# Building the decay mask of a retention kernel with two stacked float32r products instead of eight float32 ones

## The chip, the core and the metric

The kernel runs on one core of a Trainium2 chip. The core has a matrix engine (PE, with its weight loads shown apart as PEld), a vector engine (DVE), an activation engine (ACT), a general engine (POOL) and a sync engine (SP) that mostly issues DMAs; ACT issues some DMAs too. Each engine takes its instructions in program order. The metric is device time in microseconds (us) of one launch; lower is better. Chunks are counted from 0 below.

## The reference

The computation is a chain: retention (a linear attention with a decay per head), a gated feed-forward block, and four experts.

```python
# retention: B=2, H=8, S=768, D=64
gamma = 1.0 - 2.0 ** (-5.0 - np.arange(H))
for t in range(S):
    state = gamma * state + outer(k[:, :, t], v[:, :, t])
    y[:, :, t] = (1 / sqrt(D)) * q[:, :, t] @ state
# tokens: 1536, d_model 512
xn = x / rms(x) * rms_g
x = (silu(xn @ w_gate) * (xn @ w_val)) @ w_out                  # d_ff 1536, weights in float64
out = sum_e p[:, e] * (relu(x @ w1[e]) @ w2[e])                 # 4 experts, 1024 wide
```

## The kernel before

Retention runs over 12 chunks of 128 tokens (two batches of six). For a chunk the kernel computes the scores k·q of all eight heads (`scores`, L645: eight float32 matmuls, pairs of heads on the two halves of the rows), multiplies them on DVE by a decay mask (`masked`, L652), and multiplies the result with v (`mix`, L673); from chunk 1 of a batch on, `mix` also adds q times the running state (L665). At the end of `mix` the state gains k times v (L701), and ACT copies it to SBUF (L709). A chunk's q has to be multiplied by a table of decays before L665 (`prep_q`, L634, on POOL or DVE); that table, `gq`, is the product of `picks` and `q_rows` (L868), which ACT casts from constants (L859, L860), and ACT copies the product from PSUM (L870).

The mask is made once, before chunk 0. Mask[j, i] for a head is gamma^-j times gamma^i / sqrt(D) where i ≥ j. `rows` holds the two factors on a single partition; eight float32 matmuls with one row each (L832) form the outer products, and DVE multiplies them by the triangle `causal`, half of the constant `square` (L834). Around this PE also multiplies a tile of zeros by itself: eight times at the very start (L826), and eight times between the scores of chunk 0 and those of chunk 1 (L862).

The weights arrive as float64 and are turned into float32 pieces on ACT, DVE and POOL (L312 to L382) in the gaps of the retention stage. What runs when on ACT, DVE, POOL and SP there is set by a planner in Python (`Pace`): it keeps a model time `pace.now`, a clock for each engine and a cost for each operation, and at each `fill` issues the waiting tasks that fit. Whatever changes its model time or the place of a call changes which task goes to which engine, and in which order. DMAs are issued from SP in program order, and a few at the start from ACT. A DMA takes one of eight completion semaphores in turn (`DMAHW0` to `DMAHW7`), and its issue waits until the DMA before it on the same semaphore has landed.

## Time and profile before

| | |
|---|---|
| runs | 865.54, 866.02, 867.91 us; median 866.02 |
| profiled execution | span 865.7 us |
| PE busy | 853.1 us, 99% of the span |
| DVE busy | 574.6 us, 66% |
| ACT busy | 378.3 us, 44% |
| POOL busy | 280.8 us, 32% |
| mean DMA rate | 61 GB/s |

The profile is one execution. Its page gives the busy time of each engine, the span in slices, the chain of work that ended last, and groups of instructions; the timeline lists the instructions with start and duration. A float32 matmul appears as two records, so eight matmuls are "x16", and the end of a matmul in these records lies some tenths of a microsecond behind the start of the next. The column PEclk gives the granted share of PE's clock; it reads 1.00 in every stretch of this execution, but equal matmuls last twice as long in the first 14 us as after them, so which level the engine ran at is read from durations.

### The profile page before, as it was taken

Reading aid. Unit: us, or ns where it says so; the run is one execution under the profiler, and the core shown is the slowest. Engines: PE = TensorE matmul, PEld = TensorE weight load, DVE = VectorE, ACT = ScalarE, POOL = GpSimd, SP = SyncE. Lnnn points to the kernel's source line nnn. Section 1 sums busy time; section 2 is a strip of 40 time slices with the busy share of each in tenths; the row PEclk is TensorE's granted clock in tenths of the full one; section 3 lists DMA queues with packets and bytes.
Section 4 is the critical chain, followed back from the end, with each engine's and each line's share of the span. In section 5 each row is a group of like instructions: output and inputs, shape, how many; then the busy total and the mean of one; then the engine's idle time right before and its main releaser. Section 6 shows DMA issues by size and latency. Waiting matters only on the chain.

```text
span 865.7 us, 12619 instructions
## 1 busy us (share of the span) xinstructions
PE 853.1 (99%) x4731; PEld 793.1 (92%) x4731; DVE 574.6 (66%) x1054; ACT 378.3 (44%) x845; POOL 280.8 (32%) x354
## 2 busy tenths in 40 slices
PE   9999999999999999999999999999999999999998
PEld 8889999999999999889889998999889988999887
DVE  3987878979977876943565556556656566555554
ACT  3877766444354456655333233333233333333221
POOL 1366666525244458551122012012012112201000
PEclk9999999999999999999999999999999999999999
DMA  7763133211213111101011011001001101101003
GB/s 228 252 196 106 50 98 95 69 57 49 74 50 93 54 56 30 37 25 37 13 49 37 15 48 48 26 25 50 25 25 49 37 12 49 37 17 46 25 10 137
DMA packets 32749, 52.74 MB, mean 61 GB/s; under 512 B 4358, under 2 KB 13446, under 8 KB 32688
## 3 DMA queue, kind: packets, MB, share of 16 engines
q1 hardware_dynamic: 32480, 51.70, 19.1%
q8 instruction: 37, 0.61, 0.3%
q10 hardware_dynamic: 208, 0.23, 0.1%
q14 instruction: 24, 0.20, 0.1%
HBM read 48.78 MB, written 3.15 MB: 60 GB/s over the span
## 4 chain that ended last, share of the span: by engine, by line
PE 88%; DVE 5%; ACT 3%; POOL 2%; issue 1%; DMA 0%; DVEq 0%; ACTq 0%; SPq 0%; POOLq 0%
PE bank L460 41%; PE bank L1069 10%; PE bank L1070 10%; PE bank L1068 10%; PE bank L1001 3%; PE bank L1002 3%; PE bank L1000 3%; PE bank L673 1%; DVE s L553 1%; PE bank L665 1%; POOL x2Tlo L953 1%; PE bank L645 1%; DVE kept L550 1%; PE state L701 1%; DMA kn<-in_kn_dram 0%
## 5 line engine op out<-in xcount | busy, mean ns | idle before, releaser
L1076 DVE SCALAR_TENSOR_TENSOR oacc<-bank,p_sb,oacc 128x512 f32<-128x512 f32 (+1 forms) x181 | 134.8, 745 | 67.7 <-PE bank L1070 67.7
L1069 PE MATMUL bank<-plainlo,hs 128*128 128x512 f32 (+1 forms) x386 | 151.5, 392 | 0.0
L1070 PE MATMUL bank<-plainhi,hs 128*128 128x512 f32 (+1 forms) x386 | 151.5, 392 | 0.0
L1068 PE MATMUL bank<-plainhi,hs 128*128 128x512 f32 (+1 forms) x386 | 150.7, 391 | 0.0
L469 ACT COPY kept<-bank 128x384 f32<-128x384 f32 x168 | 80.5, 479 | 153.6 <-PE bank L460 151.4
L1033 DVE TENSOR_TENSOR kept<-bank,kept 128x384 f32<-128x384 f32 x96 | 53.5, 557 | 119.4 <-PE bank L460 88.2
L382 POOL TENSOR_TENSOR plainlo<-wst,plainhi 128x512 fp32r<-128x512 f32 x16 | 27.8, 1737 | 284.8 <-ACT plainhi L377 284.8
L1070 PEld LDWEIGHTS bank<-plainhi,hs 128*128 128x128 f32 x386 | 72.5, 188 | 16.1
L460 PE MATMUL bank<-x2Thi,widehi 128*128 128x384 f32 x256 | 86.2, 337 | 0.7 <-DVE kept L1033 0.7
L460 PE MATMUL bank<-x2Thi,widelo 128*128 128x384 f32 x256 | 85.7, 335 | 0.0
L460 PE MATMUL bank<-x2Tlo,widehi 128*128 128x384 f32 x256 | 85.7, 335 | 0.0
L1069 PEld LDWEIGHTS bank<-plainlo,hs 128*128 128x128 f32 x386 | 72.4, 188 | 14.3 <-POOL plainlo L382 0.3
L1068 PEld LDWEIGHTS bank<-plainhi,hs 128*128 128x128 f32 x386 | 72.4, 188 | 14.0
L382 POOL TENSOR_TENSOR widelo<-sums,widehi 128x512 fp32r<-128x512 f32 x37 | 48.4, 1308 | 112.7 <-ACT widehi L377 112.3
L1036 ACT ACTIVATE hs<-kept 128x384 fp32r<-128x384 f32 x96 | 50.4, 525 | 76.8 <-DVE kept L1033 76.8
L1001 PE MATMUL bank<-hlo,plainhi 128*128 128x384 f32 x192 | 64.3, 335 | 1.1 <-POOL hlo L558 1.0
L460 PE MATMUL bank<-xThi,widehi 128*128 128x384 f32 x192 | 64.6, 337 | 0.0
L460 PE MATMUL bank<-xThi,widelo 128*128 128x384 f32 x192 | 64.3, 335 | 0.0
L1002 PE MATMUL bank<-hhi,plainlo 128*128 128x384 f32 x192 | 64.2, 335 | 0.0
L1000 PE MATMUL bank<-hhi,plainhi 128*128 128x384 f32 x192 | 64.2, 334 | 0.0
L460 PE MATMUL bank<-xTlo,widehi 128*128 128x384 f32 x192 | 64.2, 334 | 0.0
L558 POOL TENSOR_TENSOR hlo<-s,hhi 128x384 fp32r<-128x384 f32 x44 | 47.0, 1071 | 33.5 <-ACT hhi L555 26.8
(155 smaller groups left out, 1924.2 us busy)
## 6 DMA issues: line engine op xcount, KB each, us to landing
wst<-in_moe_w_dram SPq DMA_DIRECT2D x64, 256.0 KB, 2.8
wst<-in_moe_w_gate_dram SPq DMA_DIRECT2D x12, 512.0 KB, 3.8
wst<-in_moe_w_val_dram SPq DMA_DIRECT2D x12, 512.0 KB, 3.7
wst<-in_moe_w_out_dram SPq DMA_DIRECT2D x12, 512.0 KB, 3.2
v<-in_vn_dram SPq DMA_DIRECT2D x12, 256.0 KB, 3.7
kn<-in_kn_dram SPq DMA_DIRECT2D x12, 256.0 KB, 4.1
q<-in_qt_dram SPq DMA_DIRECT2D x11, 256.0 KB, 4.3
k<-in_kt_dram SPq DMA_DIRECT2D x11, 256.0 KB, 3.0
```

The lines of the kernel that those rows point to most:

```text
L382: eng.tensor_tensor(out=at(lo), in0=t, in1=at(hi).bitcast(F32), op=ALU.subtract)
L460: nc.tensor.matmul(out=ps, lhsT=lhs, rhs=rhs, start=(first and j == i == 0), stop=(j == KH - 1 and i == 2), skip_group_check=not first,)
L469: nc.scalar.copy(out=t, in_=ps)
L1000: nc.tensor.matmul(out=ps, lhsT=whi[:, c], rhs=hi, start=(f == 0), stop=False)
L1001: nc.tensor.matmul(out=ps, lhsT=whi[:, c], rhs=lo, start=False, stop=False)
L1002: nc.tensor.matmul(out=ps, lhsT=wlo[:, c], rhs=hi, start=False, stop=(f == NF - 1))
L1033: nc.vector.tensor_tensor(out=t, in0=a, in1=t, op=ALU.add)
L1036: 0, "A", TB, lambda eng: eng.activation(out=hi, in_=t, func=AF.Relu), [pace.done(end)]
L1068: nc.tensor.matmul(out=ps, lhsT=hi[:, c], rhs=whi[:, cols], start=(f == 0), stop=False)
L1069: nc.tensor.matmul(out=ps, lhsT=hi[:, c], rhs=wlo[:, cols], start=False, stop=False)
L1070: nc.tensor.matmul(out=ps, lhsT=lo[:, c], rhs=whi[:, cols], start=False, stop=(f == NF - 1))
L1076: nc.vector.scalar_tensor_tensor(out=acc, in0=ps, scalar=pe, in1=acc, op0=ALU.mult, op1=ALU.add)
```

## The change

The two factor rows of the eight heads are split into a high and a low part and laid out on 16 rows (four pairs of heads, four products of parts); `right` holds zeros outside the pair's own columns, so one matmul over 16 rows with 512 columns gives four heads' tables at once, in float32r. DVE casts the right side in two instructions and ACT the left side in one. Only the triangle is sent early; the identity, the other half of `square`, is sent after the constants of the q table. The zero matmuls become ten before the table and three behind it; the eight between the first two chunks' scores go. The casts of `q_rows` and `picks`, and the q table of chunk 1 with `prep_q(1)`, move behind `mix(0)`. The planner's start time goes from 6.0 to 5.0.

```diff
-    WARM = 8
+    WARM = 10
+    MORE = 3
...
-        rows = [wstage.tile([P, H, CHUNK], F32, tag="wst", name=f"rows{x}")[0:1] for x in range(2)]
+        right, left = (wstage.tile([P, 2, NP, CHUNK], F32, tag="wst", name=nm)[0:NL] for nm in ("right", "left"))
+        left = left[:, :, 0]
+        rights = ap2.tile([P, 2, NP, CHUNK], F32R, tag="am", name="rights")[0:NL]
+        lefts = ap2.tile([P, NP, CHUNK], F32R, tag="xn", name="lefts")[0:NL, 0:2]
...
+        def tables(i):
+            if i < NCH - 1:
+                ps = pairs(bank())
+                nc.tensor.matmul(out=ps, lhsT=picks[:, i], rhs=q_rows, start=True, stop=True)
+                pace.matmuls(0.23)
+                nc.scalar.copy(out=gq[:, i], in_=ps)
+                gq_end[i] = pace.did("A", DM)
+            prep_q(i + 1)
...
-        for x in range(2):
-            nc.scalar.dma_start(out=rows[x], in_=c_rows[:, x])
+        nc.scalar.dma_start(out=right, in_=c_right)
+        nc.scalar.dma_start(out=left, in_=c_left)
+        nc.scalar.dma_start(out=causal, in_=c_square[:, 1])
         load(0, "q")
         load(0, "k")
-        nc.scalar.dma_start(out=square, in_=c_square)
...
         nc.scalar.dma_start(out=flat[:, NP:NP + NCH - 1], in_=c_pick)
+        nc.scalar.dma_start(out=ident, in_=c_square[:, 0])
...
+        nc.scalar.copy(out=lefts, in_=left)
+        nc.vector.tensor_copy(out=rights[:, 0], in_=right[:, 0])
+        nc.vector.tensor_copy(out=rights[:, 1], in_=right[:, 1])
         decays = [pairs(bank()) for j in range(2)]
-        for n in range(NP):
-            for j in range(2):
-                h = 2 * n + j
-                nc.tensor.matmul(out=decays[j][:, n, :], lhsT=rows[0][:, h], rhs=rows[1][:, h], start=True, stop=True)
+        for j in range(2):
+            nc.tensor.matmul(out=decays[j], lhsT=lefts[:, j], rhs=rights[:, j], start=True, stop=True)
+        for n in range(MORE):
+            nc.tensor.matmul(out=idle[:, 0, :], lhsT=S_sb[0][:, 0, :], rhs=S_sb[0][:, 0, :], start=True, stop=True)
...
-        pace.now = 6.0
+        pace.now = 5.0
...
-            if i == 0:
-
-                nc.scalar.copy(out=q_rows, in_=flat[:, 0:NP])
-                nc.scalar.copy(out=picks, in_=flat[:, NP:NP + NCH - 1])
-                for n in range(8):
-                    nc.tensor.matmul(out=idle[:, 0, :], lhsT=S_sb[0][:, 0, :], rhs=S_sb[0][:, 0, :], start=True, stop=True)
...
             mix(i)
+            if i == 0:
+                nc.scalar.copy(out=q_rows, in_=flat[:, 0:NP])
+                nc.scalar.copy(out=picks, in_=flat[:, NP:NP + NCH - 1])
+                tables(i)
```

How instructions stand before, on ACT from its first DMA to the first state copies of chunk 0 (`rows_q` is the tile that the q table's two constants are loaded to, `xn,ss` the square sum of chunk 0):

```order
L803 DMA rows_112<-in_c_rows_dram 1x1024
L803 DMA rows_113<-in_c_rows_dram 1x1024
L806 DMA square<-in_c_square_dram 128x256 [waits DMAHW2_49]
L809 DMA rows_q<-in_c_q_dram 20x512 [waits DMAHW4_49]
L810 DMA rows_q<-in_c_pick_dram 20x640 [waits DMAHW6_49]
L859 CAST q_rows<-rows_q 20x512 [waits DMAHW4_49]
L860 CAST picks<-rows_q 20x640 [waits DMAHW6_49]
L870 COPY gq<-bank 128x512 [waits PE_49]
L687 ACTIVATE xn,ss<-bank 128x512 [waits PE_49]
L689 ACTIVATE r_239<-ss,eps 128x1 [waits Activation_49]
L691 ACTIVATE vv<-ss,less 128x1 [waits Pool_49]
L709 COPY S_121<-state 64x4x64 [waits DVE_49,PE_49]
```

The same stretch of ACT in the changed kernel, up to the copy of the first q table:

```order
L817 DMA right<-in_c_right_dram 16x1024
L818 DMA left<-in_c_left_dram 16x2x128
L819 DMA square<-in_c_square_dram 128x128 [waits DMAHW1_49]
L824 DMA rows_q<-in_c_q_dram 20x512 [waits DMAHW3_49]
L825 DMA rows_q<-in_c_pick_dram 20x640 [waits DMAHW5_49]
L826 DMA square<-in_c_square_dram 128x128 [waits DMAHW7_49]
L844 CAST lefts<-left 16x256
...
L724 COPY S_123<-state 64x4x64 [waits DVE_49,PE_49]
L724 COPY S_123<-state 64x4x64
L887 CAST q_rows<-rows_q 20x512 [waits DMAHW3_49]
L888 CAST picks<-rows_q 20x640 [waits DMAHW5_49]
L660 COPY gq<-bank 128x512 [waits PE_49]
```

The cast of the left side stands behind four DMA issues, each of which waits for an earlier DMA, and the casts for the q table have moved from ahead of chunk 0's square sum to behind its state copies.

PE before, from the start to the product of the state of chunk 0:

```order
L826 MATMUL bank<-S_121 128x128 [waits DVE_49]
L826 MATMUL bank<-S_121 128x128 x7
L832 MATMUL bank<-rows_113,rows_112 128x128 [waits DMAHW7_49,DMAHW4_49]
L832 MATMUL bank<-rows_113,rows_112 128x128 x7
...
L862 MATMUL bank<-S_121 128x128 x8
L645 MATMUL bank<-q,k 128x128 [waits DMAHW1_49,DMAHW0_49]
L645 MATMUL bank<-q,k 128x128 [waits DVE_49]
L645 MATMUL bank<-q,k 128x128 x6
L868 MATMUL bank<-q_rows,picks 128x512 [waits DVE_49,Activation_49]
L673 MATMUL bank<-v,am 128x64 [waits DMAHW5_49,DVE_49]
```

PE in the changed kernel, the start and then from the product with v of chunk 0 to the scores of chunk 2:

```order
L842 MATMUL bank<-S_123 128x128 [waits DVE_49]
L842 MATMUL bank<-S_123 128x128 x9
L849 MATMUL bank<-rights,lefts 128x512 [waits DVE_49,Activation_49]
L849 MATMUL bank<-rights,lefts 128x512 [waits DVE_49]
L851 MATMUL bank<-S_123 128x128 x3
...
L688 MATMUL bank<-v,am 128x64 x6
L716 MATMUL state<-v,kn 128x128 [waits DMAHW4_49,Pool_49]
L716 MATMUL state<-v,kn 128x128 x3
L658 MATMUL bank<-q_rows,picks 128x512 [waits Activation_49]
L651 MATMUL bank<-q,k 128x128 [waits DMAHW3_49,DMAHW2_49,PE_49]
```

The first q-table product now stands between the state product of chunk 0 and the scores of chunk 2, and waits for ACT there. Elsewhere PE's rows keep their order; on DVE, ACT, POOL and SP the tasks of the planner change places through the retention stage.

## Rows read from the trace of the kernel before

**Rows 1.** The page: the span, and busy us, share and instructions of each engine.
```profile
span 865.7 us, 12619 instructions
PE 853.1 (99%) x4731; PEld 793.1 (92%) x4731; DVE 574.6 (66%) x1054; ACT 378.3 (44%) x845; POOL 280.8 (32%) x354
```
**Rows 2.** Timeline, PE: start us, us, engine, line, output and inputs, records.
```profile
1.45 3.78 PE L826 MATMUL bank<-S 128*128 128x128 f32 x16 [1.45 <-DVE S L811]
5.16 3.78 PE L832 MATMUL bank<-rows,rows 1*128 1x128 f32 x16
8.87 2.08 PE L645 MATMUL bank<-q,k 64*128 64x128 f32 x16
10.88 3.66 PE L862 MATMUL bank<-S 128*128 128x128 f32 x16
14.46 1.16 PE L645 MATMUL bank<-q,k 64*128 64x128 f32 x16
15.56 0.49 PE L868 MATMUL bank<-q_rows,picks 20*128 20x512 f32 x1
15.97 2.00 PE L673 MATMUL bank<-v,am 128*128 128x64 f32 x16
17.81 1.11 PE L701 MATMUL state<-v,kn 128*128 128x128 f32 x8
18.85 1.16 PE L645 MATMUL bank<-q,k 64*128 64x128 f32 x16
20.36 0.49 PE L665 MATMUL bank<-S,q 128*128 128x128 f32 x2
```
**Rows 3.** Timeline, the queues of ACT and SP: start and length of DMA issues.
```profile
3.98 0.38 ACTq L806 DMA_DIRECT2D square<-in_c_square_dram  x1
5.72 0.33 SPq L818 DMA_DIRECT2D g_sb<-in_moe_rms_g_dram  x1
5.95 0.29 ACTq L810 DMA_DIRECT2D rows_q<-in_c_pick_dram  x1
```
**Rows 4.** Timeline, ACT, DVE and POOL around the first two chunks.
```profile
8.65 0.62 ACT L859 CAST q_rows<-rows_q 20x512 fp32r<-20x512 f32 x1 [6.42 <-DMA rows_q<-in_c_q_dram]
10.59 0.73 ACT L860 CAST picks<-rows_q 20x640 fp32r<-20x640 f32 x1 [1.32 <-DMA rows_q<-in_c_pick_dram]
10.98 1.29 DVE L652 TENSOR_TENSOR am<-bank,mask 128x512 f32<-128x512 f32 x2 [1.14 <-PE bank L645]
16.08 0.58 ACT L870 COPY gq<-bank 128x512 f32<-128x512 f32 x1 [4.76 <-PE bank L868]
16.74 1.27 POOL L634 TENSOR_TENSOR q<-q,gq 128x512 f32<-128x512 f32 x1 [6.17 <-ACT gq L870]
19.12 0.73 ACT L709 COPY S<-state 64x256 f32<-64x256 f32 x2
```
**Rows 5.** Busy us by stretch: PE, PEld, DVE, ACT, POOL; then PEclk, DMA share, GB/s.
```profile
2.00:4.00 2.00, 2.00 (x12) 2.00 (x11) 0.00 (x0) 0.21 (x2) 0.00 (x0) 1.00 0.96 262
20.00:30.00 10.00, 10.00 (x91) 9.23 (x90) 9.32 (x17) 8.43 (x25) 4.60 (x6) 1.00 0.78 225
30.00:40.00 10.00, 9.58 (x92) 8.43 (x90) 9.09 (x19) 8.13 (x25) 2.41 (x2) 1.00 0.75 241
40.00:60.00 20.00, 18.22 (x182) 16.87 (x182) 17.09 (x37) 15.15 (x46) 11.41 (x16) 1.00 0.69 232
80.00:100.00 20.00, 19.22 (x110) 17.89 (x109) 14.52 (x25) 14.91 (x34) 15.13 (x14) 1.00 0.09 27
```
**Rows 6.** The chain that ended last, in order of time: start, us, what.
```profile
29.99 4.17 DMA kn<-in_kn_dram
34.18 0.69 DVE kn L623
38.06 0.46 PE bank L665 x2
```

## The prediction

> **What bounds the kernel now.** I read the engine totals first, then the timeline of the first 22 us, then the stretches of the retention stage, then the chain. PE is busy for 853.1 of 865.7 us [rows 1]; the reader should see there that only two things can move the time: work that leaves PE, and holes between PE's rows. The holes are few. In the stretches from 20 to 100 us that I show PE is idle for 0.42, 1.78 and 0.78 us [rows 5], 3.0 us in all. While DVE and ACT are nearly full there too (9.32 and 8.43 of 10 us from 20 to 30 us), PE still runs without a hole. So a microsecond saved at the start is worth a microsecond at the end, if nothing behind it takes it back.

> The timeline shows what the start consists of [rows 2]. Zeros run from 1.45, the eight float32 products of the table from 5.16, the scores of chunk 0 from 8.87, zeros again from 10.88, and the scores of chunk 1 from 14.46. Equal work has two durations: the scores of chunk 0 take 2.08 us and those of chunk 1 1.16. [...] What PE did before the rise: the zeros at the start (3.78 us, all rows) did not bring it, the one-row products behind them neither, and it came at the end of scores and zeros over the full height, which ran from 8.87 without a hole.

> I follow two marks. T is the end of chunk 0's state product: 17.81 + 1.11 = 18.92 us. M is the start of chunk 1's product with the state, 20.36 us [rows 2]. From M on both kernels do the same PE work in the same order, so the shift of M is the first estimate of the change.

> **The first part: up to the table's products.** Ten zeros instead of eight: the eight took 5.16 − 1.45 = 3.71 us, two more at half clock cost 2 × 0.43 (two records of 3.71/16 each, less the first fill), so PE is through at 6.0. But the products wait for `lefts`, and its cast stands on ACT behind four DMA issues. The third of them waits for v of chunk 0 to land; SP's issue behind that same wait starts at 5.72 [rows 3]. The new constants are 72 KB larger (64 + 16 against 8), at 262 GB/s [rows 5] 0.27 us: 5.99. Then come that issue (0.29), the identity's issue (0.38, as the square's) [rows 3] and the cast. A cast of 512 columns takes 0.62 and one of 640 0.73 [rows 4], 0.85 ns a column, so 256 columns take 0.62 − 0.22 = 0.40. Sum 7.06, with the hop to PE 7.1. PE stands idle for 1.1 us here: the zeros do not run unbroken. Without the DMA delay it would be 0.8, with twice the delay 1.4. The two casts of `rights` on DVE cost nothing: DVE has no work before the table, and even at 0.7 us each from 3.6 on they end before 6.0.

> Each float32r product has 512 columns in one pass; the nearest row is the q table's product, 0.49 us at full clock [rows 2], so at half clock I take 0.5 each (bounds 0.43 and 0.98, the latter if all of it doubles): 8.1. Three zeros: 1.35, to 9.45. Scores of chunk 0 at half clock: 2.05, to 11.5, against 10.95 before. Scores of chunk 1 follow at once, since the eight zeros between are gone: 13.55 at half clock, against 15.6 before. The masked scores on DVE take 1.29 [rows 4] and end near 12.8, under the scores of chunk 1. The product with v and the state product take 18.92 − 15.97 = 2.95 at full clock.

> When does the clock rise? The rows show one rise, at 14.4, after scores and zeros without a hole; no row fixes it for another sequence. If it rises at 14.4 again, chunk 0's product runs its first part slowly and T is 17.0. If it rises already during the ten zeros, T is 13.9 (below). If it rises at 13.6, as chunk 0's product starts, T is 13.55 + 2.95 = 16.5. I take 16.5: it lies between the two, near the one rise that a row shows, and a little ahead of it, as scores and zeros stand closer together now.

> **The second part: the q table moved behind chunk 0.** Before, the two casts ran at 8.65 and 10.59 in ACT's empty time, and q of chunk 1 was ready at 16.74 + 1.27 = 18.01 [rows 4], 2.3 us ahead of M. Now they stand behind the state copies, on the path. From T: the state copies end 19.12 + 0.73 − 18.92 = 0.93 later; the casts add 0.62 and 0.73, to 2.28. Up to there PE has nothing: its next instruction is the table's product, which waits for `picks`, and behind it stand the scores of chunk 2 that could run. From the product's start to the end of POOL's multiplication it is 18.01 − 15.56 = 2.45 us. So M is T + 4.75 with the hop. In that time PE does the table's product, the scores of chunk 2 and the second table, some 2 us; the other 2.8 it is idle. Before, M was T + 1.44. This step costs 3.3 us.

> M comes to 16.5 + 4.75 = 21.25, 0.9 us later than before. The early saving of 2.4 us in T (float32r for float32, eight zeros fewer between the scores) is eaten by the wait for ACT and POOL.

> **The third part: the order behind it.** The planner's model time starts 1.0 lower, and tasks change engine, and the order on DVE, ACT, POOL and SP differs through the whole retention stage. No row shows what the new order costs. It can at best close the holes that the rows show, −3.0 us, and I allow as much on the other side. In the chain, PE's wait at 38.06 goes back to a DVE multiplication that waited for a DMA issued at 29.99 [rows 6]; that DMA waits for a state product, so it moves with PE and does not bind harder. I take 0, the value between, as DVE's and ACT's total work stays within a few instructions of 1054 and 845.

> **The sum** goes against the profiled execution: 865.7 + 0.9 = 866.6. The median of the runs, 866.02, lies 0.3 above that execution, so the forecast is 866.9 us. Its own range, with T from 16.0 to 17.5 and the order at ±1.5, is 865 to 869.

> **The rivals.**

> The clock rises early. For it: PE now runs ten full-height matmuls, 4.6 us, before anything else. Against: 3.78 us of the same did not do it [rows 2], and the 1.1 us hole comes behind. If it does, the products end at 7.1 + 0.65 (two of 512 columns at full clock), three zeros add 0.7, the scores 1.1 each: chunk 0's to 9.55, chunk 1's to 10.65. Now DVE's masked scores are late: 9.6 + 1.3 = 10.9. T is 10.95 + 2.95 = 13.9, M 18.65, 1.7 us earlier than before: 864.3 us. [...]

> The clock falls again: the case on the slower side. Its place is the hole behind T. The largest hole in the rows before is part of 1.78 us in 20 us [rows 5], and the clock held over it; here PE would stand for 2.3 us with nothing, do 2 us, and stand again. The point from which it decides is whether this suffices for a fall. Price: PE ran at half clock for about 5.5 us of full-height work before the rise at 14.4 [rows 2]; at half speed that is 2.75 us lost. 866.9 + 2.8 = 869.7 us. [...]

> The order of the tasks decides. If the new order closes all holes of [rows 5], the time is 866.9 − 3.0 = 863.9, with the early clock 861.3; if it doubles them, 869.9. For the first: chunk 1's and 2's multiplications are spread differently over DVE and POOL, and POOL, which is busy for 4.60 of 10 us from 20 on, gets more of them. Against: the engine that is full is DVE, and it keeps nearly all of its work.

> The left side is not late. If the cast does not wait behind v's landing, PE goes on at 6.0, T and M come 1.1 us earlier, and the time is 865.8 us. Against it stands the order on ACT, and that the issue of the pick constants started right after its wait before [rows 3].

> **How the numbers follow.** Forecast 0.38; early clock 0.28; fall of the clock 0.07; better order 0.11; worse order 0.09; left side on time 0.07. About 0.3%, 2.6 us, is what a measurement of this kernel can tell from no change: faster means below 863.4, slower above 868.6. Faster: most of the better order (0.08), and the part of the early clock that meets a better order (0.08), 0.16. Slower: the fall (0.07), most of the worse order (0.07), the tail of the forecast (0.02), 0.16. The rest, 0.68, is no change. The range leaves out a tenth on either side: 863.3 to 869.3 us.

> **What would show it.** Right: a hole of about 1 us on PE ahead of the two 512-column products; scores of chunks 0 and 1 back to back; a hole of about 2.3 us behind chunk 0's state product, ended by ACT's cast of `picks`, and a short one ahead of M, ended by POOL; M within 1 us of 21.25. Wrong: M before 20 us; scores of chunk 0 at 1.16 us instead of 2.08; the products starting at 6.0; matmuls behind M at twice their duration; or PE's idle time from M to 100 us differing from before by more than 1.5 us.

## The result, and the profile after

The changed kernel takes 873.23 us (median of 6 runs, 871.51 to 877.98) against 865.78 (6 runs, 865.41 to 867.91): a ratio of 1.0086, 95% interval 1.0069 to 1.0103. It is slower by 7.45 us, outside the range of 863.3 to 869.3 and on the side that had 0.16. The profiled executions differ by 872.9 − 865.7 = 7.2 us. Of 53 later runs of the kernel before, 30 took 863.6 to 865.7 us and 23 took 867.0 to 868.1, and its profiled execution, with its span of 865.7, belongs with the longer ones, at about 867.5.

PE's timeline in the changed kernel, from the start to the scores of chunk 4 (start us, us, engine, line, output and inputs, records, and in brackets the idle time before and what ended it):

```profile
1.45 4.64 PE L842 MATMUL bank<-S 128*128 128x128 f32 x20 [1.45 <-DVE S L827]
7.47 1.21 PE L849 MATMUL bank<-rights,lefts 16*128 16x512 f32 x2 [1.39 <-ACT lefts L844]
8.62 1.65 PE L851 MATMUL bank<-S 128*128 128x128 f32 x6
10.20 3.79 PE L651 MATMUL bank<-q,k 64*128 64x128 f32 x32
13.91 2.09 PE L688 MATMUL bank<-v,am 128*128 128x64 f32 x16
15.84 1.11 PE L716 MATMUL state<-v,kn 128*128 128x128 f32 x8
...
19.20 0.50 PE L658 MATMUL bank<-q_rows,picks 20*128 20x512 f32 x1 [2.25 <-ACT picks L888]
19.63 1.16 PE L651 MATMUL bank<-q,k 64*128 64x128 f32 x16
...
21.72 0.79 PE L680 MATMUL bank<-S,q 128*128 128x128 f32 x2 [0.39 <-POOL q L640]
...
26.89 2.02 PE L716 MATMUL state<-v,kn 128*128 128x128 f32 x8
...
29.70 1.86 PE L651 MATMUL bank<-q,k 64*128 64x128 f32 x16
...
36.12 1.16 PE L651 MATMUL bank<-q,k 64*128 64x128 f32 x16
```

Against [rows 2]: T, the end of chunk 0's state product, is 15.84 + 1.11 = 16.95 instead of 18.92, and then come both holes of the prediction, 2.25 and 0.39 us. M is 21.72 instead of 20.36. Behind M every row up to about 31 us is slow. The state product of chunk 1 lasts 2.02 us against 1.11 for chunk 0's, the same eight records. The stretches say it plainly (busy us of PE, PEld, DVE, ACT and POOL, then granted clock, DMA share, GB/s):

```profile
14.00:21.00 7.00, 4.75 (x42) 4.09 (x42) 2.23 (x5) 4.18 (x12) 0.60 (x1) 1.00 0.96 310
21.00:31.00 10.00, 9.61 (x49) 8.95 (x50) 4.42 (x8) 4.41 (x13) 1.95 (x2) 0.50 0.20 59
31.50:41.50 10.00, 9.89 (x89) 9.08 (x88) 7.67 (x16) 7.57 (x21) 4.98 (x5) 1.00 0.74 225
```

From 21 to 31 us the granted clock is 0.50, and PE gets through 49 records where the next ten us hold 89. PE is nearly always busy there; the loss is in the speed, not in holes.

Where the 7.2 us arise is read from equal PE rows of the two traces. Scores before, of chunks 3, 4 and 11:

```profile
24.57 1.16 PE L645 MATMUL bank<-q,k 64*128 64x128 f32 x16
...
30.29 1.16 PE L645 MATMUL bank<-q,k 64*128 64x128 f32 x16
...
68.94 1.16 PE L645 MATMUL bank<-q,k 64*128 64x128 f32 x16
```

and after, chunk 11 (chunks 3 and 4 stand above, at 29.70 and 36.12):

```profile
75.51 1.16 PE L651 MATMUL bank<-q,k 64*128 64x128 f32 x16
```

| place | before | after | shift | added since the row above |
|---|---|---|---|---|
| M | 20.36 | 21.72 | 1.36 | 1.36 |
| scores of chunk 4 | 30.29 | 36.12 | 5.83 | 4.47, at half clock |
| scores of chunk 11 | 68.94 | 75.51 | 6.57 | 0.74 |
| span | 865.7 | 872.9 | 7.2 | 0.6 |

From M to the scores of chunk 4, before and after:

```profile
20.36:30.29 9.93, 9.93 (x91) 9.23 (x90) 9.29 (x17) 8.45 (x25) 4.60 (x6) 1.00 0.79 234
21.72:36.12 14.40, 14.40 (x90) 13.54 (x90) 6.94 (x14) 6.39 (x19) 4.02 (x4) 0.67 0.34 91
```

PE has no idle time in either stretch, and does the same work (the one record more before is the end of the q-table product that starts at 19.94), so the 4.47 us between them are speed alone. So 4.5 of the 7.2 us are the fall of the clock. 1.4 are the shift of M: T comes 1.97 us earlier, but the way from T to M, with the wait for the q table, is 3.33 us longer. 1.3 come later.

### The profile page after: what moved, and what is told of

The parts are those of the page before. It is cut to its first block, busy times and chain, and to the rows that moved or that the text cites. A ratio compares the mean times of both kernels' runs of the same rounds, so it can differ in the third digit from the quotient of the medians.

```text
span 872.9 us, 12584 instructions
## 1 busy us (share of the span) xinstructions
PE 855.6 (98%) x4711; PEld 794.0 (91%) x4711; DVE 573.5 (66%) x1051; ACT 379.7 (44%) x846; POOL 283.4 (32%) x359
## 3 DMA queue, kind: packets, MB, share of 16 engines
q1 hardware_dynamic: 32480, 51.70, 18.9%
## 4 chain that ended last, share of the span: by engine, by line
PE 85%; DVE 5%; ACT 4%; issue 3%; POOL 2%; DMA 0%; SPq 0%; DVEq 0%; ACTq 0%; POOLq 0%
PE bank L463 39%; PE bank L1080 10%; PE bank L1081 10%; PE bank L1079 10%; PE bank L1012 3%; PE bank L1013 3%; PE bank L1011 3%; PE bank L688 2%; PE bank L680 1%; DVE s L556 1%; POOL x2Tlo L964 1%; DVE kept L553 1%; PE state L716 1%; PE bank L651 1%; ACT kept L472 1%
```

## The experiments

Each kernel was timed beside the kernel before. Ratios are against it, with 95% intervals. The theory after the result: the hole behind T lets the clock fall, and that costs 4.5 us. Its rivals: the new order of the planner's tasks, the first hole, or the products themselves.

**The hole filled.** Ten zero matmuls stand ahead of the first q-table product; nothing else changes.

```diff
             if i < NCH - 1:
                 ps = pairs(bank())
+                for n in range(10 if i == 0 else 0):
+                    nc.tensor.matmul(out=ps[:, 0, :], lhsT=S_sb[1][:, 0, :], rhs=S_sb[1][:, 0, :], start=True, stop=True)
```

> The changed kernel, with ten zero matmuls put into PE's hole behind the state product of chunk 0, ahead of the table's product that waits for ACT. Theory (the hole lets the clock fall, and the fall costs 4.5 us): nothing on ACT or POOL moves, so M stays near 21.7 us, but PE runs at full clock from there on, the scores of chunk 3 start near 25.9 instead of 29.7, and the time falls by about 4.5 us, to about 868.7. Rival (the new order of the planner's tasks costs the 7 us): the zeros change nothing, about 873.

Measured: 870.33 us (7 runs, 868.4 to 873.14), ratio 1.0048 (1.0028 to 1.0069). PE's timeline:

```profile
15.77 1.11 PE L718 MATMUL state<-v,kn 128*128 128x128 f32 x8
16.72 2.40 PE L659 MATMUL bank<-S 128*128 128x128 f32 x20
19.13 0.50 PE L660 MATMUL bank<-q_rows,picks 20*128 20x512 f32 x1
...
21.65 0.49 PE L682 MATMUL bank<-S,q 128*128 128x128 f32 x2 [0.50 <-POOL q L640]
...
24.38 1.11 PE L718 MATMUL state<-v,kn 128*128 128x128 f32 x8
...
25.85 1.16 PE L651 MATMUL bank<-q,k 64*128 64x128 f32 x16
```

The decisive point came out: M is unchanged (21.65), the state product takes 1.11 us again, and the scores of chunk 3 start at 25.85, within 0.1 of the forecast; the zeros, which compute nothing, take the half clock away from this stretch (granted 1.00 from 21 to 31 us). The median fell by 2.9 us instead of 4.5. In the profiled execution, the longest of the seven (873.14 us), the clock fell later, after a stretch with other holes, of 0.60 and 1.33 us among them:

```profile
46.00:52.00 6.00, 4.07 (x41) 3.60 (x40) 5.50 (x13) 4.21 (x14) 3.02 (x4) 1.00 0.85 311
52.00:58.70 6.70, 6.70 (x39) 6.15 (x38) 4.81 (x10) 4.46 (x12) 2.36 (x3) 0.50 0.27 80
```

That the other six runs lost the missing part in the same way is not shown; their mean granted clocks lie between 0.994 and 0.999.

**The table back.** Casts and first table ahead of the product with v of chunk 0, as before the change, but without the eight zeros.

```diff
+            if i == 0:
+                nc.scalar.copy(out=q_rows, in_=flat[:, 0:NP])
+                nc.scalar.copy(out=picks, in_=flat[:, NP:NP + NCH - 1])
             if i + 1 < NS:
                 scores(i + 1)
-                if i:
-                    tables(i)
+                tables(i)
...
-            if i == 0:
-                nc.scalar.copy(out=q_rows, in_=flat[:, 0:NP])
-                nc.scalar.copy(out=picks, in_=flat[:, NP:NP + NCH - 1])
-                tables(i)
```

> The changed kernel, with the two casts and the first q table put back to their old place, ahead of the product with v of chunk 0 (without the eight zeros that stood there). Theory: no hole behind the state product, so no fall of the clock and no wait for POOL: T near 17.4, M near 18.9, 1.5 us earlier than before the change; the time is 864 to 867, the rest of the spread being the planner's order. Rival (the order costs it, or the hole at the start does): 870 or more.

Measured: 865.93 us (12 runs, 863.92 to 870.42), ratio 0.9997 (0.9982 to 1.0012). The whole loss is gone with this one edit, the new products, the new zeros, the later identity and the start time of 5.0 still in place:

```profile
16.22 1.11 PE L716 MATMUL state<-v,kn 128*128 128x128 f32 x8
17.26 1.16 PE L651 MATMUL bank<-q,k 64*128 64x128 f32 x16
18.36 0.50 PE L658 MATMUL bank<-q_rows,picks 20*128 20x512 f32 x1
18.78 0.49 PE L680 MATMUL bank<-S,q 128*128 128x128 f32 x2
```

T is 17.33 and M 18.78, with no hole. M is 1.58 earlier than in the profiled execution before, and the profiled span 864.2, 1.5 less than 865.7. The medians do not show that gain: the profiled execution before stands for some 867.5 us, while the median of its kernel is 865.63 here, and the mean granted clock of some runs of this kernel goes down to 0.992, which I read as falls; these runs have no traces. The edit also moves the planner's tasks, so by itself it does not part the hole from their order; the filled hole does, as nothing but PE's zeros changes there.

**The left side on DVE.**

```diff
-        nc.scalar.copy(out=lefts, in_=left)
         nc.vector.tensor_copy(out=rights[:, 0], in_=right[:, 0])
         nc.vector.tensor_copy(out=rights[:, 1], in_=right[:, 1])
+        nc.vector.tensor_copy(out=lefts, in_=left)
```

> The changed kernel, with the cast of the left side on DVE behind the two casts of the right side, instead of on ACT behind four DMA issues. Theory: the first hole goes, the products start near 6.1, T and M come about 1.2 us earlier, but the hole behind T stays and with it the fall of the clock: 871 to 873. Rival (it is the first hole that matters for the clock later): no fall, below 868.

Measured: 872.75 us (6 runs, 870.75 to 873.33), ratio 1.0069 (1.0052 to 1.0086), as the theory had it.

```profile
6.02 0.98 PE L849 MATMUL bank<-rights,lefts 16*128 16x512 f32 x2
...
7.79 1.16 PE L651 MATMUL bank<-q,k 64*128 64x128 f32 x16
...
12.46 1.11 PE L716 MATMUL state<-v,kn 128*128 128x128 f32 x8
15.81 0.50 PE L658 MATMUL bank<-q_rows,picks 20*128 20x512 f32 x1 [2.24 <-ACT picks L888]
...
23.63 2.02 PE L716 MATMUL state<-v,kn 128*128 128x128 f32 x8
```

Here the zeros run into the products, and in this execution the clock is up before the scores of chunk 0 (1.16 us). T is 13.57, 5.35 earlier than before, and still the kernel is slow: the hole behind T is the same 2.24 us, and the state product of chunk 1 is at half clock again (2.02 us; the mean granted clock is 0.70 from 14 to 31 us). A high clock ahead of the hole did not help here.

**Both.** The last two edits together, with the diffs above.

> Both of the last two edits: table and casts at their old place, left side cast on DVE. Theory: no hole in the first 22 us, M near 17.8, 2.5 us earlier than before the change: 863 to 865, faster than both kernels. Rival (the planner's order takes it back): 866 or more.

Measured: 868.31 us (12 runs, 864.54 to 872.24), ratio 1.0022 (1.0002 to 1.0041). The theory's number was missed, and the rival's, 866 or more, came out. But the trace shows another cause than the planner's order, which was the rival's. I had left out that with an early clock PE can be ahead of its data:

```profile
6.75 1.16 PE L651 MATMUL bank<-q,k 64*128 64x128 f32 x16
9.31 1.16 PE L651 MATMUL bank<-q,k 64*128 64x128 f32 x16 [1.40 <-DMA k<-in_kt_dram]
11.22 0.79 PE L658 MATMUL bank<-q_rows,picks 20*128 20x512 f32 x1 [0.75 <-ACT picks L878]
11.94 3.67 PE L688 MATMUL bank<-v,am 128*128 128x64 f32 x16
15.41 2.02 PE L716 MATMUL state<-v,kn 128*128 128x128 f32 x8
```

Two holes, 1.40 and 0.75 us with 1.16 between them, and behind them the product with v lasts 3.67 us instead of 2.00. In this execution shorter holes than the one behind T brought the clock down too.

**The casts alone back.** The two casts return to ACT's empty time; the table's product and what follows stay behind chunk 0.

```diff
+            if i == 0:
+                nc.scalar.copy(out=q_rows, in_=flat[:, 0:NP])
+                nc.scalar.copy(out=picks, in_=flat[:, NP:NP + NCH - 1])
...
             if i == 0:
-                nc.scalar.copy(out=q_rows, in_=flat[:, 0:NP])
-                nc.scalar.copy(out=picks, in_=flat[:, NP:NP + NCH - 1])
                 tables(i)
```

> The changed kernel, with the two casts of the q table's constants put back to their old place in ACT's empty time; the table's product, its copy and the multiplication on POOL stay behind chunk 0. Theory: the hole behind T shrinks from 2.25 us to almost nothing and the one ahead of M to about 0.5, M comes to 19.5 instead of 21.7, the clock mostly holds: 866 to 869. Rival (it is the place of the table's product, through the planner's order, that costs): 871 or more.

Measured: 868.7 us (12 runs, 865.39 to 871.49), ratio 1.0029 (1.0014 to 1.0045), inside the theory's numbers: 4.5 us of the 7.45 are gone by moving two instructions of ACT, 1.35 us of work. The profiled execution (868.0 us) is not quite what the theory said:

```profile
7.24 0.73 PE L849 MATMUL bank<-rights,lefts 16*128 16x512 f32 x2 [1.38 <-ACT lefts L844]
...
18.27 0.49 PE L680 MATMUL bank<-S,q 128*128 128x128 f32 x2 [1.00 <-POOL q L640]
```

The hole behind T is gone, but the one ahead of M is 1.00 us instead of 0.5, and M comes at 18.27, not 19.5. The clock was up before the products (0.73 us instead of 1.21) and fell behind the first hole, though PE worked without a break from 7.24 on:

```profile
9.00:12.00 3.00, 3.00 (x30) 3.00 (x30) 2.15 (x4) 1.34 (x2) 1.04 (x1) 0.50 0.99 317
```

Six of the twelve runs have a mean granted clock of 0.996 or lower. What the place of the product costs beside the casts is not shown.

**The table's place alone, on the kernel before.** Old products, old zeros, start time 6.0; the two casts, the table's product, its copy and `prep_q(1)` behind `mix(0)`.

```diff
-                nc.scalar.copy(out=q_rows, in_=flat[:, 0:NP])
-                nc.scalar.copy(out=picks, in_=flat[:, NP:NP + NCH - 1])
                 for n in range(8):
...
-                if i < NCH - 1:
+                if 0 < i < NCH - 1:
...
-                prep_q(i + 1)
+                if i:
+                    prep_q(i + 1)
...
             mix(i)
+            if i == 0:
+                nc.scalar.copy(out=q_rows, in_=flat[:, 0:NP])
+                nc.scalar.copy(out=picks, in_=flat[:, NP:NP + NCH - 1])
+                ps = pairs(bank())
+                nc.tensor.matmul(out=ps, lhsT=picks[:, i], rhs=q_rows, start=True, stop=True)
...
+                prep_q(1)
```

> The kernel before, with one part of the change alone: the two casts and the first q table moved behind chunk 0 (old products, old zeros, old start time). Theory: a hole of 2.3 us behind T, M at T + 4.75, about 23.2 (2.8 us later than before), and the clock falls in that hole for some 10 us, 4.5 us more: about 873. Rival (the hole costs only its own length): 868 to 869. Second rival (the table's products, not the table's place, made the change slow): no change, 866.

Measured: 875.23 us (4 runs, 871.27 to 877.64), ratio 1.0118 (1.0096 to 1.0140). This part alone makes the kernel as slow as the whole change did (the two intervals overlap), 2 us above the theory's 873, and both rivals are out.

```profile
7.48 1.16 PE L645 MATMUL bank<-q,k 64*128 64x128 f32 x16
...
13.73 1.11 PE L701 MATMUL state<-v,kn 128*128 128x128 f32 x8
17.09 0.50 PE L882 MATMUL bank<-q_rows,picks 20*128 20x512 f32 x1 [2.24 <-ACT picks L880]
...
19.60 0.80 PE L665 MATMUL bank<-S,q 128*128 128x128 f32 x2 [0.50 <-POOL q L634]
...
24.78 1.88 PE L701 MATMUL state<-v,kn 128*128 128x128 f32 x8
```

The same holes, 2.24 and 0.50 us, and half clock behind them again, here for some 7 us:

```profile
19.50:26.40 6.90, 6.80 (x32) 6.80 (x33) 4.40 (x8) 1.93 (x6) 0.05 (x1) 0.51 0.08 32
```

This execution, at 871.27 us, is the shortest of the four. M − T is 4.76, as forecast; M itself is 19.60 and not 23.2, because here the clock was up before the scores of chunk 0. So an early rise occurs with the old zeros and products too.

**The casts back and the left side on DVE.** The diffs of the third and the fifth experiment together.

> The last but one, with the left side cast on DVE too. Theory: the first hole goes as well, the clock can rise during the ten zeros, and T comes to 13 to 16; the table's product stands behind chunk 0, so PE does not wait for its constants before that: 862 to 866, where the clock holds. Rival (short holes between the scores of chunks 0 and 1 and ahead of M let the clock fall): 867 to 869.

Measured: 866.42 us (12 runs, 865.33 to 872.93), ratio 1.0014 (0.9998 to 1.0031): slightly above the theory's range, below the rival's. In the profiled execution M comes at 16.77, 3.6 us earlier than before, and the clock holds (granted 1.00 up to 60 us; the product with v of chunk 0 takes 2.00 us, its state product 1.11); the span, 864.4, keeps only 1.3 of that.

```profile
9.80 1.16 PE L651 MATMUL bank<-q,k 64*128 64x128 f32 x16 [1.19 <-DMA k<-in_kt_dram]
...
16.77 0.49 PE L680 MATMUL bank<-S,q 128*128 128x128 f32 x2 [0.15 <-POOL q L640]
```

So these runs give no length of a hole at which the clock falls: it fell behind 2.25 and 0.39 us, behind 1.40 and 0.75, and behind 1.38, and it held over 1.19 here and over 1.36 in the changed kernel (at 60.48, below).

**Zeros in the holes.** The kernel with both edits, with six zeros ahead of the scores of chunk 1 and three ahead of the first table.

```diff
             if i == 0:
...
+                for n in range(6):
+                    nc.tensor.matmul(out=idle[:, 0, :], lhsT=S_sb[0][:, 0, :], rhs=S_sb[0][:, 0, :], start=True, stop=True)
...
                 ps = pairs(bank())
+                for n in range(3 if i == 0 else 0):
+                    nc.tensor.matmul(out=ps[:, 0, :], lhsT=S_sb[1][:, 0, :], rhs=S_sb[1][:, 0, :], start=True, stop=True)
```

> Table and casts at their old place, left side cast on DVE, and the two holes that this left (1.40 us ahead of the scores of chunk 1, 0.75 ahead of the first table) filled with six and three zero matmuls. Theory: the clock, once up, does not fall in the first 20 us; a late rise costs up to 1.9 us more for the zeros at half clock: 864 to 867, with a smaller spread than the same kernel without these zeros (864.5 to 872.2). Rival (falls elsewhere in the retention stage make the spread): spread and median as without, 868.

Measured: 864.94 us (11 runs, 864.54 to 866.25), ratio 0.9989 (0.9979 to 1.0000), inside the theory's numbers. The spread shrinks from 7.7 us to 1.7, and all eleven runs show a mean granted clock of 1.000, where without these zeros it was 0.990 to 1.000. So no fall is on record in any of them; when the clock rose first, this mean does not tell, as the column reads 1.00 ahead of the first rise. It is the fastest kernel here by its median, ahead of the kernel before by 0.1%, just at the edge of what the interval tells.

## Why the prediction was wrong, point by point

*The first part, up to the products, held.* The zeros ended at 6.09 (forecast 6.0), the products waited for `lefts` (1.39 us idle; 1.1), and the cast stood behind the issues of the pick constants and the identity, took 0.41 us (0.40) and let the products start at 7.47 (7.1). These rows of ACT and its queue in the changed kernel show the chain that the forecast added up:

```profile
6.28 0.30 ACTq L825 DMA_DIRECT2D rows_q<-in_c_pick_dram  x1
6.61 0.36 ACTq L826 DMA_DIRECT2D square<-in_c_square_dram  x1
7.02 0.41 ACT L844 CAST lefts<-left 16x256 fp32r<-16x256 f32 x1 [4.79 <-DMA square<-in_c_square_dram]
```

The scores of chunks 0 and 1 ran back to back and T came at 16.95 (16.5). That the clock rose about where the forecast put it is in part luck: with the casts alone back the same zeros and products are issued, and there it was up before the products (0.73 us for both against 1.21). The 0.5 for each product at half clock and the 0.65 for both at full clock were estimates of mine.

*The second part held.* M − T is 4.77 (4.75), with 2.25 and 0.39 us of idle time (2.28 and some 0.5). The step cost what was said: M shifted by 1.36, forecast 0.9.

*The step that failed is the choice between this forecast and the rival "the clock falls again".* The place, the hole behind T, was named; I gave it 0.07, on the ground that the clock had held over holes before (granted 1.00 from 20 to 60 us [rows 5]). But the largest hole in the rows I leaned on is less than 1 us, and the forecast's own was 2.3:

```profile
47.10 0.63 PE L749 MATMUL bank<-square,xn 128*128 128x128 f32 x4 [0.87 <-DVE xn L727]
```

In the trace the clock fell, and with it came one of the prediction's own signs of being wrong, matmuls behind M at twice their duration (2.02 us against 1.11). In six of six runs of the changed kernel the mean granted clock is 0.994 or lower: five at 0.994, the profiled one among them, with 0.50 from 21 to 31 us, and one at 0.986. I take the others to have fallen at least as long, which is not shown, as they have no traces. In the profiled executions 2.25 us with 0.39 behind it were enough for a fall here, and 1.40 with 0.75 in the kernel with both edits.

*The price of the fall was mis-sized.* Forecast 2.75 us, from the 5.5 us of full-height work at half clock ahead of the rise at the start; measured 4.47, since the half clock lasted for some 10 us of nearly full PE work (granted 0.50 from 21 to 31 us, PE busy for 9.61). It lasted for some 7 us in the kernel with the hole filled (0.50 from 52 to 58.7) and in the kernel before with the table moved (0.51 from 19.5 to 26.4), and for 3 us or a little more with the casts alone back (0.50 from 9 to 12), so one price does not fit all falls. Even this rival's own number, 869.7, lies 3.5 us below the measured time.

*The third part*, the planner's order at 0, missed 0.74 us up to chunk 11 and 0.6 behind it. PE's idle time from M to 100 us, 2.95 us against 3.02 before, hardly moved, so the rival in which the order doubles the holes is out. One place can be seen: the product with the state for chunk 7 waits for ACT for 1.36 us, where before it waited 0.73 (first row).

```profile
53.95 0.46 PE L665 MATMUL bank<-S,q 128*128 128x128 f32 x2 [0.73 <-ACT S L709]
60.48 0.46 PE L680 MATMUL bank<-S,q 128*128 128x128 f32 x2 [1.36 <-ACT S L724]
```

The kernel with the table back, start time 5.0, waits 0.74 there, and the kernel before with only the table moved, start time 6.0, 1.33. So it is the table's place, not the start time, that goes with the longer wait. The order was not tried apart from the rest, and where the last 0.6 us arise was not found.

*The sum's anchor was off.* I took the profiled execution to be 0.3 below the median. The time lies 1.8 above the span (874.73 and 872.9 for the profiled execution after; later runs of the kernel before with the span 865.7 took about 867.5), so that execution before was a run of about 867.5, at the upper end of its runs; forecast and median did not belong together by 1.5 us.

*The early clock* does occur: three of the kernels with the left side on DVE show it (scores of chunk 0 in 1.16 us, at 6.75 to 7.79), and one with the old zeros; with the casts alone back the clock was up at the products (0.73 us), and fell again (0.50 from 9 to 12 us). Where the hole behind T stayed, it was no gain: with the left side alone on DVE, T came 5.35 us earlier and the kernel stayed 0.7% slower.

Left open: why the clock stayed low for some 10 us of dense PE work behind the hole, and for 3 to 7 us elsewhere; what decides whether a hole of 1.2 to 1.4 us brings a fall; and what the order alone costs.

## What to carry to other kernels

A hole on PE had two prices here: its length, and what the clock lost behind it. In the profiled execution 2.25 us of waiting and a hole of 0.39 behind it cost 4.5 us more, so casts and copies that PE will wait for belong into their engine's empty time, early, even where the product that uses them comes late. When an instruction is moved on an in-order engine, list what now stands ahead of it, DMA issues with their waits included, and who waits behind: here the cast of the left side started at 7.02 us, behind issues at 6.28 and 6.61, and PE stood idle for 1.39. Where the hole can't be closed, zero matmuls can fill it: in the kernel with both edits nine of them took the spread of the times from 7.7 to 1.7 us.
